# Attention and two MLPs on one core: the start made anew, the first MLP's products begun pair by pair, and idle products on TensorE

## The chip, the cores and the metric

The kernel runs on one core of one Trainium2 chip. The metric is the device time of one execution in microseconds, median of several runs; before the change it is 845.37 us (three runs, 844.19 to 846.44). The core's engines are TensorE (PE; PEld is its weight load), VectorE (DVE), ScalarE (ACT), GpSimd (POOL) and SyncE (SP, which here only issues DMAs). TensorE writes to PSUM, which has eight banks of 128 partitions by 512 f32 columns.

## The reference

Four batches, eight heads, 576 positions, head size 64. Scores get a bias from a running sum of gates and a causal mask; then come two MLPs on the 2304 tokens.

```python
def _attn_ref(q, k, v, s):
    B, H, S, D = q.shape                     # 4, 8, 576, 64
    scores = np.matmul(q, k.transpose(0, 1, 3, 2)) / np.sqrt(D)
    cum = np.cumsum(np.maximum(s, 0.0), axis=-1)
    bias = -(cum[:, :, :, None] - cum[:, :, None, :])
    scores = np.where(causal, -1e9, scores + np.minimum(bias, 0.0))
    attn = softmax(scores)
    return np.matmul(attn, v)

def _moe_ref(x, w_in, w_out, g_ln):          # 512 -> 1024 -> 512
    h = x @ w_in
    solu = h * softmax(h)
    return layernorm(solu) * g_ln @ w_out

def _moe2_ref(x, w_in, w_out):               # 512 -> 2048 -> 512
    h = x @ w_in
    return (h * np.clip(h + 3.0, 0.0, 6.0) / 6.0) @ w_out
```

Weights come as float64, which the kernel reads as pairs of 32-bit words and decodes on ScalarE and VectorE to a rounded high part and a low part. MLP products are made of three: high by high, low by high, high by low.

## The kernel before

The whole program is planned. Every step is entered in a list by `plan.add` with its engine, an estimated duration, what it reads and writes, buffers that it takes from a ring (`new`), a PSUM bank, and sometimes steps after whose start it may begin (`after`). `Plan.emit` schedules the list: each engine takes, of the steps that are ready by the estimates, the one that was entered first; a step that needs a PSUM bank waits until one is free. The instructions are then written engine by engine in that order, and on the chip each engine and each DMA queue works strictly in it.

Batch 0 is done in head pairs, 0 to 3. `load_qk` loads a pair's q and k (two DMAs of 144 KB each) on SP's queue; `prep_whole` transposes them on TensorE (12 products with the identity, L440) and copies them out (q on ScalarE at L445, k on VectorE at L447). `gate_rows` loads the gates s of all heads, takes the running sum on VectorE (L278 to L282), splits it in a high and a low part and writes the parts and rows of ones to the DRAM tensor `rows_d` (L286); `load_gates` reads four rows for each head back into the lower half of a 128-partition tile `whole`, whose other rows there are zero (L427). A score group of `qk_whole` (L583) is four f32 products: gate rows of the two heads of the pair (64 partitions each), then q by k of the two heads (64 partitions each). Scores of the first 256 positions ("early", t = 0, 1) come first, pair by pair (`pairs(False)`); the others ("late", t = 2, 3, 4) follow (`pairs(True)`).

Softmax: VectorE adds the mask and takes the maximum (L531), ScalarE takes the exponential (L543), VectorE the reciprocal of the sum (L639, L640), GpSimd scales (L644). TensorE transposes the result (L678), ScalarE or VectorE copies it out (L682), TensorE multiplies it by V (`av`, L707), and the product is copied to the x tile (L714). The first MLP works on tiles of 128 tokens: `ffn1_x` rounds a whole x tile to xh (VectorE, L794) and subtracts to xl (GpSimd, L798); `ffn1_h` adds up 24 products (L812: two halves f of w_in by four chunks kk by three); then come statistics, transposes (L878) and `ffn1_out` with w_out (L899). Chunk kk of x is what head pair kk gives. Tiles 0 and 1 are just the first 256 positions of batch 0.

`split64` loads and decodes one piece of a weight; for w_in (8 pieces, `load_w_in`) the load (512 KB) is issued from ScalarE's queue (L317), after the piece two before it is done; the steps of decoding are L323 (ACT), L327 and L331 (DVE), the high part L338 (DVE, first four) or L340 (ACT), the low part L347 (POOL). The 16 pieces of w_out follow in the same way. From batch 1 on, scores come from stacks of 128 rows in one f32r pass (L610), whose gate rows also come from `rows_d`. The second MLP (L1071, L1102) ends the program.

Of the kernel before, what the change touches and what calls it, by code (L numbers as in the profile page):

```python
# [37 lines left out]
HI_IN = 4  # L38
# [3 lines left out]
LAG = 2  # L42
DELAY = 3.5
# [4 lines left out]
class Plan:  # L48
# [45 lines left out]
    def emit(self):  # L94
# [17 lines left out]
        banks = [(0.0, b) for b in range(8)]  # L112
# [51 lines left out]
        for _, i in sorted(order):  # L164
            self.ops[i][2]()
# [23 lines left out]
def kernel(ctx, tc, q, k, v, s, w_in, w_out, g_ln, w2_in, w2_out, out):  # L189
# [53 lines left out]
    w_out_part(False)  # L243
# [21 lines left out]
    def gate_rows():  # L265

        s_sb = ap2.tile([P, S], F32, tag="y4", name="s_sb")[:NH]
        one = ap2.tile([P, S], F32, tag="y4", name="one")[:NH]
        cum = ap2.tile([P, NQ, 2, D], F32, tag="V", name="cum").rearrange("p c j d -> p (c j d)")[:NH, :S]  # L270
        pos = ap2.tile([P, PT_COLS], F32, tag="pt", name="pos", bufs=PT).bitcast(F32R)[:NH, : 2 * S]
        neg = ap2.tile([P, PT_COLS], F32, tag="pt", name="neg", bufs=PT).bitcast(F32R)[:NH, : 2 * S]

        def load():
            nc.sync.dma_start(out=s_sb, in_=s.rearrange("b h s -> (b h) s"))

        def sums():
            nc.vector.tensor_scalar_max(s_sb, s_sb, 0.0)  # L278
            nc.vector.tensor_tensor_scan(cum, one, s_sb, 0.0, ALU.mult, ALU.add)
            nc.vector.tensor_copy(pos[:, :S], cum)  # L280
            nc.vector.tensor_sub(pos[:, S:], cum, pos[:, :S].bitcast(F32))
            nc.vector.tensor_scalar_mul(neg, pos.bitcast(F32), -1.0)  # L282

        def put(i, r, src):
            dst = rows_d[:, i, r::2, :]
            nc.sync.dma_start(out=dst, in_=src)  # L286

        def zeros(j):
            whole_t[j] = ap1.tile([P, 4, S], F32, tag=f"stack{j}", name=f"whole{j}")
            nc.gpsimd.memset(whole_t[j][:, 2:4, :], 0.0)  # L290

        plan.add("SP", 0.45, load, writes=["s"], lag=2.0)
        plan.add("POOL", 2.2, lambda: nc.gpsimd.memset(one, 1.0), writes=["one"])
        plan.add("DVE", 3.0, sums, reads=["s", "one"], writes=["c"])
        ones = one.unsqueeze(1).to_broadcast([NH, 2, S])
        both = lambda c: c.bitcast(F32).rearrange("p (i s) -> p i s", i=2)
        for i, r, src, key in ((1, 0, both(pos), "c"), (0, 1, both(neg), "c"), (0, 0, ones, "one"), (1, 1, ones, "one")):
            plan.add("SP", 0.55, lambda i=i, r=r, src=src: put(i, r, src), reads=[key], writes=[f"rows/{i}{r}"], lag=2.0)
        for j in range(2):
            plan.add("POOL", 1.3, lambda j=j: zeros(j), writes=[f"zeros{j}"], new=[(f"stack{j}", 1, f"whole{j}")])  # L300

    def split64(plan, pool, src, hi, lo, name, key, scale=None, bufs=1, ring="", raws64=2, after=(), hi_dve=False, on_dve=(), behind=None, needs=(), home=()):
# [6 lines left out]
        w = f"raw_{name}"  # L309

        def load():
            T["raw"] = raw = pool_at().tile([P, n, 2], I32, tag="raw64", name=w, bufs=raws64)
# [8 lines left out]
        def high():  # L321
            T["a"] = pool_at().tile([P, n], F32, tag="dec_a", name=f"a_{name}", bufs=bufs)
# [870 lines left out]
```

## Time and profile before

| what | value |
|---|---|
| median of three runs | 845.37 us |
| profiled execution, its own time | 846.22 us |
| its span in the trace | 844.40 us |
| TensorE busy | 818.4 us (97%) |
| VectorE busy | 438.5 us (52%) |
| ScalarE busy | 399.4 us (47%) |
| GpSimd busy | 209.4 us (25%) |

The profile is that of one execution. An engine counts as busy while an instruction runs; the ends of TensorE's products are modelled, so shares close to 100% mean "no gap", not "at its peak". The page also cuts the span in 40 slices of 21.1 us each and gives the busy share of each in tenths, and the granted clock of TensorE in tenths of full speed. The chain of waits is followed back from the last instruction: at each step to what released it.

### The profile page before, as it was taken

What the parts mean: (1) busy time and instruction counts of PE and PEld (TensorE: products, weight loads), DVE (VectorE), ACT (ScalarE), POOL (GpSimd) and SP (SyncE); (2) the same over time, 40 slices, a digit from 0 to 9 for tenths busy, and PEclk for the clock granted to TensorE, in tenths of its full rate; (3) what the DMA queues carried; (4) which work ended last, traced back from release to release, by engine and by line L of the source; (5) the groups of instructions that cost most, each with busy time, mean ns of one, the idle gap of its engine ahead of it and who ended that gap; (6) DMA issues with size and microseconds to landing.
All of it is one profiled execution on the core that took longest, in us unless ns stands there. A gap on an engine that the chain in (4) does not pass through costs nothing.

```text
span 844.4 us, 13546 instructions
## 1 busy us (share of the span) xinstructions
PE 818.4 (97%) x4864; PEld 689.5 (82%) x4864; DVE 438.5 (52%) x1125; ACT 399.4 (47%) x928; POOL 209.4 (25%) x309
## 2 busy tenths in 40 slices
PE   4899999999999999999999999999999999999997
PEld 3565588898898889888999999998888888888886
DVE  4677887746855574749826982234222322222221
ACT  2575767755765575736636662244222422232222
POOL 1563643424632363327402220000000000000000
PEclk9899999999999999999999999999999999999999
DMA  6753596755646455223605640012000300010001
GB/s 172 180 152 110 120 209 152 176 120 130 129 118 137 98 129 120 65 99 121 193 32 194 214 148 1 1 62 88 1 1 0 100 1 0 1 50 1 0 1 50
DMA packets 95938, 77.52 MB, mean 92 GB/s; under 512 B 64288, under 2 KB 78112, under 8 KB 95872
## 3 DMA queue, kind: packets, MB, share of 16 engines
q1 hardware_dynamic: 93568, 68.27, 31.9%
q10 hardware_dynamic: 2304, 8.39, 3.1%
q8 instruction: 38, 0.62, 0.3%
q14 instruction: 28, 0.23, 0.1%
HBM read 45.38 MB, written 10.03 MB: 66 GB/s over the span
## 4 chain that ended last, share of the span: by engine, by line
PE 91%; DVE 4%; DMA 1%; POOL 1%; issue 1%; ACT 0%; POOLq 0%; DVEq 0%; SPq 0%; ACTq 0%
PE bank L1071 24%; PE bank L1102 24%; PE bank L899 11%; PE bank L812 11%; PE bank L707 6%; PE bank L678 5%; PE bank L610 5%; PE bank L583 3%; PE bank L878 2%; PE bank L473 1%; DMA stack<-HL12k 1%; DVE y L531 0%; DMA rows_d<-neg 0%; POOL y L626 0%; POOL y L644 0%
## 5 line engine op out<-in xcount | busy, mean ns | idle before, releaser
L1071 PE MATMUL bank<-x2h,w 128*128 128x512 f32 (+1 forms) x640 | 185.3, 370 | 0.0
L1102 PE MATMUL bank<-w,gh 128*128 128x512 f32 x576 | 178.8, 393 | 0.0
L1079 DVE SCALAR_TENSOR_TENSOR g<-g,bank 128x512 f32<-128x512 f32 (+1 forms) x80 | 50.6, 633 | 206.3 <-ACT g L1075 206.0
L1071 PEld LDWEIGHTS bank<-x2h,w 128*128 128x128 f32 x640 | 118.7, 188 | 18.7
L1075 ACT ACTIVATE g<-bank 128x512 f32<-128x512 f32 (+1 forms) x80 | 44.5, 556 | 178.8 <-PE bank L1071 178.7
L1102 PEld LDWEIGHTS bank<-w,gh 128*128 128x128 f32 x576 | 107.9, 188 | 21.9
L1071 PE MATMUL bank<-x2l,w 128*128 128x512 f32 (+1 forms) x320 | 118.5, 370 | 0.0
L1102 PE MATMUL bank<-w,gl 128*128 128x512 f32 x288 | 111.9, 391 | 0.0
L531 DVE CUSTOM_DVE_ANT_0 y<-bank,mask 96x288 f32<-96x288 f32 (+4 forms) x168 | 74.6, 467 | 57.3 <-PE bank L610 37.7
L543 ACT ACTIVATE y<-y,nmax 128x256 f32<-128x256 f32 (+4 forms) x140 | 83.4, 597 | 41.4 <-DVE nmax L531 29.9
L626 POOL TENSOR_SCALAR y<-y,rsum 128x128 f32<-128x128 f32 (+4 forms) x120 | 68.1, 589 | 103.7 <-DVE rsum L622 48.5
L899 PE MATMUL bank<-zh,w_out_h 128*128 128x256 f32 x288 | 82.8, 288 | 0.0
L899 PE MATMUL bank<-zl,w_out_h 128*128 128x256 f32 x288 | 81.2, 282 | 0.0
L899 PE MATMUL bank<-zh,w_out_l 128*128 128x256 f32 x288 | 81.2, 282 | 0.0
L1087 DVE TENSOR_TENSOR gl<-g,gh 128x512 fp32r<-128x512 f32 (+1 forms) x80 | 53.7, 671 | 43.4 <-ACT gh L1083 42.6
L1083 ACT CAST gh<-g 128x512 fp32r<-128x512 f32 (+1 forms) x80 | 46.2, 577 | 48.2 <-DVE g L1079 48.1
L1071 PEld LDWEIGHTS bank<-x2l,w 128*128 128x128 f32 x320 | 60.0, 188 | 8.3
L1102 PEld LDWEIGHTS bank<-w,gl 128*128 128x128 f32 x288 | 54.1, 188 | 12.1
L812 PE MATMUL bank<-w_in_h,xh 128*128 128x512 f32 x144 | 61.6, 428 | 0.8 <-DVE xh L794 0.8
L610 PE MATMUL bank<-stack 128*96 128x288 f32 (+4 forms) x288 | 57.8, 317 | 1.2 <-DMA stack<-HL12k 0.8
L812 PE MATMUL bank<-w_in_h,xl 128*128 128x512 f32 x144 | 57.4, 399 | 0.6 <-POOL xl L798 0.6
L812 PE MATMUL bank<-w_in_l,xh 128*128 128x512 f32 x144 | 57.4, 398 | 0.0
(220 smaller groups left out, 1360.9 us busy)
## 6 DMA issues: line engine op xcount, KB each, us to landing
raw_w2i<-in_moe_w_in_dram SPq DMA_DIRECT2D x16, 512.0 KB
raw_w2o<-in_moe_w_out_dram SPq DMA_DIRECT2D x16, 512.0 KB
rawq<-in_q_dram SPq DMA_DIRECT2D x32, 144.0 KB
rawk<-in_k_dram SPq DMA_DIRECT2D x32, 144.0 KB
x_d<-x2s SPq DMA_DIRECT2D x36, 128.0 KB
out_dram<-ob SPq DMA_DIRECT2D x18, 256.0 KB
raw_wi<-in_moe_w_in_dram ACTq DMA_DIRECT2D x8, 512.0 KB
raw_wo<-in_moe_w_out_dram ACTq DMA_DIRECT2D x8, 512.0 KB
```

The lines of the kernel that those rows point to most:

```text
L531: nc.vector.tensor_tensor_reduce(out=ys[h, t][:n, c0:c1], in0=bank(key)[:n, : c1 - c0], in1=mask[:n, 480 + n - w + c0 : 480 + n - w + c1], ...
L543: nc.scalar.activation(out=y[:n], in_=y[:n], func=AF.Exp, bias=nmax[:n, h, t : t + 1], scale=-1.0, accum_out=sums[:n, h, t : t + 1])
L610: nc.tensor.matmul(bank(key)[:n, : c1 - c0], lhsT=ss[:, 2 - 2 * m, ST[t] : w], rhs=ss[:, 3 - 2 * m, c0:c1], start=(m == 0), stop=(m == 1))
L626: nc.gpsimd.tensor_scalar(ys[h, t][:n], ys[h, t][:n], rsum[:n, h, t : t + 1], 1.0, ALU.mult, ALU.mult)
L707: nc.tensor.matmul(bank(key)[j * D : (j + 1) * D, lo - c0 : c1 - c0], lhsT=vs[v_key(p, a)][:n, jj, j, :], rhs=pts[pt_key(2 * p + j, a)][:n ...
L812: nc.tensor.matmul(bank(key), lhsT=xs[i][m // 2][:, kk, :], rhs=(w_in_l if m == 1 else w_in_h)[:, kk, f * 512 : (f + 1) * 512], start=(kk ...
L899: nc.tensor.matmul(bank(key)[:, : 2 * P], lhsT=w_out_at(w, kk)[:, m * P : (m + 1) * P], rhs=z[:, kk, :], start=(kk == 0 and i == 0), stop= ...
L1071: nc.tensor.matmul(bank(key)[:, :w], lhsT=wt[:, a, 0, c * P : (c + 1) * P], rhs=x[:, c, :w], start=(c == 0 and i == 0), stop=(c == KDM - 1 ...
L1079: nc.vector.scalar_tensor_tensor(out=gg, in0=gg, scalar=6.0, in1=bank(key)[:, :w], op0=ALU.min, op1=ALU.mult)
L1083: nc.scalar.copy(gh[:, :w], gg[:, :w])
L1087: nc.vector.tensor_sub(gl[:, :w], gg[:, :w], gh[:, :w].bitcast(F32))
L1102: nc.tensor.matmul(bank(key), lhsT=g_t[ci, m][1 + i // 2][:, t * P : (t + 1) * P], rhs=w2[m][:, i % 2, 1, :], start=(m == 0 and i == 0), s ...
```

## The change

1. **Gates of batch 0 on the chip.** The first eight heads' s come by a DMA that is the first on ScalarE's queue. `places` makes, from the identity, a small matrix that has two ones for each head; four f32 products (`own`, 288 columns, 8 rows) spread s to two rows in each of four strips of 32 partitions. ScalarE clips (`clip`), VectorE takes the running sum (`total`) and turns the two rows of a strip to sum and one; ScalarE writes the key rows (`keys`). The sum is no longer split in high and low. One tile `whole` holds the gates of two pairs, and a head's gate product has 32 partitions. `load_gates` is gone. The `rows_d` tensor, which batches 1 to 3 need, is made later by `all_rows`, after `po3_0` (the early product of pair 3 with V) has begun.
2. **q and k of pairs 1, 2, 3** are loaded at the start, into buffers that the first MLP uses later (`raw_home`), so without waiting for the pair before.
3. **w_in** is loaded by SP's queue, into the home of w_out's first part and decoded in place there; w_out's decoding begins when that is done. The high part is VectorE's for the first two pieces, not four.
4. **x of tiles 0 and 1.** For batch 0's early part `av` no longer copies to x; ScalarE rounds each pair's product to xh straight from PSUM and VectorE subtracts to xl. `ffn1_h` of tiles 0 and 1 waits for chunk kk alone, not for the whole tile.
5. **Idle products.** `emit` fills 60% of TensorE's planned idle time from 1 to 24 us of the plan with products of the identity by itself (taken as bf16, 256 columns), 46 in all, into bank 7, which the plan gives to others only from 24 us on; nothing reads them.
6. Estimates of score groups and loads are changed, which moves the order everywhere.

The core of the diff:

```diff
-HI_IN = 4
+HI_IN = 2
+FILL_FROM, FILL_TO, FILL_N, FILL = 1.0, 24.0, 256, 0.6
...
-        banks = [(0.0, b) for b in range(8)]
+        banks = [(0.0, b) for b in range(7)] + [(FILL_TO, 7)]
...
-        for _, i in sorted(order):
-            self.ops[i][2]()
+        todo = [(start, i, self.ops[i][2]) for start, i in order]
+        free = FILL_FROM
+        for start, i in sorted((start, i) for start, i in order if self.ops[i][0] == "PE" and start < FILL_TO):
+            todo += [(free + k * fill_us, -1, fill) for k in range(int(FILL * (start - free) / fill_us))]
+            free = max(free, start + self.ops[i][1])
+        for _, _, f in sorted(todo, key=lambda x: x[:2]):
+            f()
...
+        def own(i, c):
+            n = S // 2
+            nc.tensor.matmul(bank(f"own{i}_{c}")[:, :n], lhsT=spread[:, i].rearrange("h g r -> h (g r)"), rhs=s_first[:, c * n : (c + 1) * n], start=True, stop=True)
...
+            nc.scalar.activation(out=cums[i][:, c * n : (c + 1) * n], in_=bank(f"own{i}_{c}")[:, :n], func=AF.Relu)
...
+            nc.vector.tensor_tensor_scan(cums[i], one, cums[i], 0.0, ALU.mult, ALU.add)
+            nc.vector.tensor_scalar(whole_t[i][:, 2, :], cums[i], at[:, 1:2], at[:, 0:1], ALU.mult, ALU.add)
...
+            nc.scalar.activation(out=whole_t[i][:, 3, :], in_=cums[i], func=AF.Identity, scale=at[:, 0:1], bias=at[:, 2:3])
...
+        plan.add("ACT", 0.4, lambda: nc.scalar.dma_start(out=s_first, in_=s[0]), writes=["s0"], lag=2.3)
...
-        return whole_t[p % 2][j * D : (j + 1) * D, 2:4, :]
+        r = (2 * (p % 2) + j) * (P // 4)
+        return whole_t[p // 2][r : r + P // 4, 2:4, :]
...
-            issue = nc.sync if behind is None else nc.scalar
+            issue = nc.sync if behind is None or raw_at else nc.scalar
...
+            if b == 0 and a == 0:
+                for i in range(2):
+                    def high(i=i, key=key):
+                        nc.scalar.copy(xs[i][0][:, hp, :], bank(key)[:, i * P : (i + 1) * P])
+                    def low(i=i, key=key):
+                        nc.vector.tensor_sub(xs[i][1][:, hp, :], bank(key)[:, i * P : (i + 1) * P], xs[i][0][:, hp, :].bitcast(F32))
...
-        plan.add("PE", 0.7, mm, reads=[f"xs{i}/h", f"xs{i}/l"] + W_IN[kk, f], writes=[key],
+        plan.add("PE", 0.7, mm, reads=[f"xs{i}/{x}{kk if i < 2 else ''}" for x in "hl"] + W_IN[kk, f], writes=[key],
...
+    def keep_clock():
+        x = ident.bitcast(BF16)
+        nc.tensor.matmul(banks[7][:, :FILL_N], lhsT=x[:, :P], rhs=x[:, :FILL_N], start=True, stop=True)
```

What this does to the order is seen at three places. The line numbers are those of each kernel: L512, L661, L756, L785 and L903 of the change are L440, L583, L678, L707 and L812 of before.

TensorE's first work before: the transposes of pair 0's q and k, the first score group, then pair 1's q.

```order
L440 MATMUL bank0_96<-ident_60,rawq0_119 128x96 x3
L440 MATMUL bank1_97<-ident_60,rawq0_119 128x96 x3
L440 MATMUL bank2_98<-ident_60,rawk0_122 128x96 x3
L440 MATMUL bank3_99<-ident_60,rawk0_122 128x96 x3
L583 MATMUL bank4_100<-whole0_125 128x128
L583 MATMUL bank5_101<-whole0_125 128x128
L583 MATMUL bank4_100<-HL0_137 128x128
L583 MATMUL bank5_101<-HL0_137 128x128
L440 MATMUL bank6_102<-ident_60,rawq1_147 128x96 x3
```

The same place in the change, from the last of the first ten idle products (L1268) on; L287 is `own`.

```order
L1268 LDWEIGHTS ident_60
L1268 MATMUL bank7_101<-ident_60 128x256
L287 MATMUL bank0_94<-start_t_109 128x288
L287 MATMUL bank1_95<-start_t_109 128x288
L287 MATMUL bank2_96<-start_t_109 128x288
L287 MATMUL bank3_97<-start_t_109 128x288
L512 MATMUL bank4_98<-ident_60,rawq0_119 128x96 x3
L512 MATMUL bank5_99<-ident_60,rawq0_119 128x96 x3
```

The spreading products and idle products have come ahead of pair 0's transposes; the first score group now stands behind the transposes of pairs 0 and 1 and of half of pair 2's q.

TensorE where the first MLP begins, before: the last early transposes (L678) and late scores are done, pair 3's product with V (L707) is made, and the products of tile 0 follow one another.

```order
L707 MATMUL bank5_101<-pt6a_496,V3a_420 64x256
L707 MATMUL bank5_101<-pt7a_501,V3a_420 64x256
L707 MATMUL bank5_101<-pt6a_496,V3a_420 64x128
L707 MATMUL bank5_101<-pt7a_501,V3a_420 64x128
L473 MATMUL bank0_96<-ident_60,rawq4_354 128x96 x3
L473 MATMUL bank2_98<-ident_60,rawq4_354 128x96 x3
L812 MATMUL bank5_101<-w_in_h_82,xh0_555 128x512
L812 MATMUL bank5_101<-w_in_l_83,xh0_555 128x512
L812 MATMUL bank5_101<-w_in_h_82,xl0_556 128x512
```

In the change, behind pair 3's early scores (L661, `whole1`):

```order
L661 MATMUL bank2_96<-whole1_208 128x256
L661 MATMUL bank3_97<-whole1_208 128x256
...
L903 MATMUL bank5_99<-w_in_h_82,xh0_388 128x512
L903 MATMUL bank5_99<-w_in_l_83,xh0_388 128x512
L903 MATMUL bank5_99<-w_in_h_82,xl0_389 128x512
L756 MATMUL bank1_95<-ident_60,yf2_303 128x128 x3
L756 MATMUL bank6_100<-ident_60,yf3_304 128x128 x3
L661 MATMUL bank7_101<-whole0_163 128x384
L661 MATMUL bank1_95<-whole0_163 128x384
L661 MATMUL bank7_101<-HL0_152 128x384
L661 MATMUL bank1_95<-HL0_152 128x384
```

Three products of tile 0, for chunk 0 alone, stand between the early and the late scores of pair 0; the others of tiles 0 and 1 follow in threes between score groups, transposes and products with V, all ahead of the first transposes of the late part.

SP's queue at the start, before (L275 loads s, L286 writes `rows_d`, L427 reads it):

```order
L275 DMA s_sb_110<-in_s_dram 32x576
L395 DMA rawq0_119<-in_q_dram 96x6x64 x2
L395 DMA rawk0_122<-in_k_dram 96x6x64 x2
L286 DMA rows_d_71<-one_111 32x2x576 x2
L286 DMA rows_d_71<-pos_113 32x2x576
L286 DMA rows_d_71<-neg_114 32x2x576
L395 DMA rawq1_147<-in_q_dram 96x6x64 x2
```

In the change (`rawqz`, `rawkz` hold pair 1's and then pair 2's):

```order
L466 DMA rawq0_119<-in_q_dram 96x6x64 x2
L466 DMA rawk0_122<-in_k_dram 96x6x64 x2
L466 DMA rawqz_131<-in_q_dram 96x6x64 x2
L466 DMA rawkz_132<-in_k_dram 96x6x64 x2
L366 DMA raw_w_in0_142<-in_moe_w_in_dram 128x1024
```

Pair 1's loads have moved up directly behind pair 0's, and the first w_in piece stands on this queue, ahead of pair 2's.

## Rows read from the trace of the kernel before

**Rows 1.** The page, busy share by engine, and slices of 21.1 us.
```profile
PE 818.4 (97%) x4864; PEld 689.5 (82%) x4864; DVE 438.5 (52%) x1125; ACT 399.4 (47%) x928; POOL 209.4 (25%) x309
...
PE   4899999999999999999999999999999999999997
...
PEclk9899999999999999999999999999999999999999
```

**Rows 2.** Stretches: length, busy us of each engine, granted clock, DMA share, GB/s.
```profile
0.00:15.00 15.00, 2.39 (x12) 1.89 (x13) 7.48 (x9) 2.99 (x5) 4.20 (x13) 1.00 0.73 199
15.00:31.00 16.00, 14.47 (x80) 10.74 (x82) 7.56 (x33) 7.90 (x28) 6.69 (x10) 0.83 0.64 145
31.00:62.25 31.25, 28.18 (x171) 18.44 (x172) 23.55 (x77) 20.07 (x53) 17.15 (x20) 0.92 0.65 169
62.25:109.30 47.05, 45.11 (x321) 29.15 (x320) 38.16 (x109) 31.27 (x75) 23.18 (x33) 1.00 0.50 123
109.30:844.40 735.10, 728.25 (x4286) 629.25 (x4284) 361.75 (x898) 337.19 (x768) 158.13 (x234) 1.00 0.32 83
```

**Rows 3.** Chain of waits up to 34 us: start, duration, what (f32 products count twice).
```profile
0.72 2.00 DMA s_sb<-in_s_dram
...
5.19 1.36 DVE cum L279
...
8.61 4.17 DMA rows_d<-neg
...
12.93 1.93 DMA whole<-rows_d
...
15.00 1.57 PE bank L583 x8
...
17.73 2.01 PE bank L583 x8
...
30.96 1.48 PE bank L707 x8
...
33.24 0.50 PE bank L440 x6
33.74 2.75 PE bank L583 x16
```

**Rows 4.** Timeline up to 23 us: start, duration, engine, line, operation.
```profile
1.14 0.29 POOL masks.py:199 TENSOR_SCALAR_AFFINE_SELECT ident<-ident 128x128 f32<-128x128 f32 x1
...
4.66 1.19 PE L440 MATMUL bank<-ident,rawq 96*128 96x96 f32 x6 [4.66 <-DMA rawq<-in_q_dram]
...
5.41 0.89 ACT L445 ACTIVATE HL<-bank 128x288 f32<-128x288 f32 x2 [3.20 <-PE bank L440]
...
22.44 0.59 PE L583 MATMUL bank<-HL 64*128 64x256 f32 x4
```

**Rows 5.** Chain of waits again, later pieces.
```profile
54.69 1.27 POOL xl L798
...
56.01 6.25 PE bank L812 x19
62.25 2.17 PE bank L678 x24
...
79.39 1.14 PE bank L583 x8
80.54 0.90 PE bank L812 x3
...
82.58 0.38 PE bank L678 x3
82.97 0.73 PE bank L812 x3
...
171.12 2.89 PE bank L899 x24
```

**Rows 6.** Timeline, the first product with w_out.
```profile
109.34 0.28 PE L899 MATMUL bank<-zh,w_out_h 128*128 128x256 f32 x1
```

More of the change, by code (lines that the diff above doesn't have):

```diff
@@ L292, in gate_rows @@
[L292 to L298, printed above, removed]
@@ L299, in gate_rows @@
-        for j in range(2):
-            plan.add("POOL", 1.3, lambda j=j: zeros(j), writes=[f"zeros{j}"], new=[(f"stack{j}", 1, f"whole{j}")])
-    def split64(plan, pool, src, hi, lo, name, key, scale=None, bufs=1, ring="", raws64=2, after=(), hi_dve=False, on_dve=(), behind=None, needs=(), home=()):
+        one = ap2.tile([P, S], F32, tag="y4", name="one")
+        start_t = ap2.tile([P, PT_COLS], F32, tag="pt", name="start_t", bufs=PT)[:H]
+        s_first = start_t[:, :S]
+        at = const.tile([P, 3], F32, name="at")
@@ new lines, in gate_rows, with gates @@
+        plan.add("POOL", 1.9, lambda: nc.gpsimd.memset(one, 1.0), writes=["one"])
+        plan.add("DVE", 1.4, places, writes=["at"])
+        def gates(i):
+            for c in range(2):
+                key = f"own{i}_{c}"
+                plan.add("PE", 0.3, lambda i=i, c=c: own(i, c), reads=["s0", "at"], writes=[key], bank=key)
+                plan.add("ACT", 0.45, lambda i=i, c=c: clip(i, c), reads=[key], writes=[f"cum{i}/{c}"], new=[("e", 2, f"cum{i}")] if c == 0 else [])
+            plan.add("DVE", 2.0, lambda i=i: total(i), reads=[f"cum{i}/0", f"cum{i}/1", "one", "at"], writes=[f"gates{i}/q", f"cum{i}/t"], new=[(f"stack{i}", 1, f"whole{i}")])
+            plan.add("ACT", 0.7, lambda i=i: keys(i), reads=[f"cum{i}/t"], writes=[f"gates{i}/k"])
@@ L304, in split64 @@
+    def split64(plan, pool, src, hi, lo, name, key, scale=None, bufs=1, ring="", raws64=2, after=(), hi_dve=False, on_dve=(), behind=None, needs=(), home=(), raw_at=None, a_at=None):
         n = 512
@@ L366, in load_w_in, with raw_at @@
         c %= KDM
[L367 to L368 removed]
+        i = c + f.start // 128
+        def raw_at():
+            if i < 2:
+                w1_raw[i] = w1p.tile([P, KFF - LATE_OUT, DM], F32, tag=f"w_out_{'hl'[i]}0", name=f"raw_w_in{i}").rearrange("p c n -> p (c n)")
+            o = (i % 4 // 2) * 1024
+            return w1_raw[i % 2][:, o : o + 1024].bitcast(I32).rearrange("p (n w) -> p n w", w=2)
+        first = [lambda: plan.add("ACT", 0.0, lambda: None, writes=["raws/"], new=[("wout", 1, "raws")])] if i == 0 else []
+        return first + split64(plan, dec, w_in[c * P : (c + 1) * P, f], w_in_h[:, c, f], w_in_l[:, c, f], f"wi{c}_{f.start // 512}", "win",
+                               behind=[], hi_dve=i < HI_IN, raw_at=raw_at, a_at=lambda: w1_raw[i % 2][:, 2048:])
     def load_w_out(c):
@@ L546, in exps @@
             plan.add("DVE", 0.2, both, reads=[f"nmax{h}_{NQ}"], writes=[f"nmax{h}_{t}"])
-        plan.add("ACT", act(w, 0.46), exp, reads=[f"nmax{h}_{t}"] + [f"{y_key(h, t)}/{c0}" for c0, _, _ in pieces], writes=[f"{y_key(h, t)}/e", f"sums{h}_{t}"])
+        plan.add("ACT", act(w, 0.46), exp, reads=[f"nmax{h}_{t}"] + [f"{y_key(h, t)}/{c0}" for c0, _, _ in pieces], writes=[f"{y_key(h, t)}/e", f"sums{h}_{t}"],
+                 after=[f"rawx/{H - 1}_1/e"] if h < H and ST[t] >= CUT else [])
     def pieces_of(t):
```

177 lines of the change are left out of this document (117 added, 60 removed).

## The prediction

> **What bounds the kernel now.** I read the page's busy shares and the granted clock in slices first [rows 1]: TensorE is nearly full from the third slice on, so what can be gained lies at the start. The table of stretches [rows 2] splits it. Up to 15.0 us TensorE works 2.39 us; from 15 to 31 it works 14.47 of 16, from 31 to 62.25 28.18 of 31.25, from 62.25 to 109.3 45.11 of 47.05, and after that 728.25 of 735.1. So it idles 19.1 us before 109.3 and 6.85 after it. Part of the busy time is half speed: granted 0.83 and 0.92 in the second and third stretch are 2 x 0.17 x 16 = 5.4 and 2 x 0.08 x 31.25 = 5.0 us at 1.2 GHz.
>
> The chain of waits [rows 3] says why the start is late: s lands at 2.72, its running sum is taken on VectorE (1.36 us), the parts are written to DRAM (4.17 us) and read back (1.93 us), and only at 15.00 the first score products run. [...] I take that as the low level; by 22.44, where two of those 256-column products took 0.59 [rows 4], it is over. The first pair's product with V begins at 30.96. The first MLP begins when its whole x tile is rounded and split: the xl of 1.27 us at 54.69 releases the long run of MLP products at 56.01 [rows 5]. I use three marks: first product with V (30.96), first transposes of the second half (62.25), first products with w_out (109.34) [rows 3, 5, 6].
>
> **Up to the first product with V.** Removed are the trip through DRAM, its four DMAs ahead of pair 1's q on SP's queue, and the w_in DMAs beside it. Added is a chain on the chip. s of batch 0 goes first on ScalarE's queue; in before 2.00 us passed from issue to landing [rows 3], so 2.7. The identity is made at 1.14 + 0.29 = 1.43 [rows 4]. Ten idle products stand ahead of the first real one. No bf16 product is in the trace; the nearest are 24 of 256 columns in 2.89 us [rows 5], 0.12 each, 0.24 at the low level: TensorE is through with them at 2.7 to 3.9. I take 3.9, where the clock was low in before. The four products that spread s (288 columns, f32) have no row: if they ran as the paired score products do, 288 columns cost 0.26 (high) or 0.56 (low); alone, at most twice that, so 0.26 to 1.13. I take 0.8, the middle towards the low level: the second ends at 5.5, the fourth at 7.1. Then ScalarE's clip (0.45, half of the 0.89 for two of 288 columns [rows 4]), the scan (1.36 [rows 3]) and a scaled copy on VectorE (between 0.45 and 1.36; 0.75): query rows at 8.1. The key rows are on ScalarE behind pair 1's q copies. TensorE first transposes q0, k0 and q1, three times 0.50 to 1.19, with a filler product between: 9.9. Two copies 0.89, key rows 0.7: the first score product at 11.5 instead of 15.00 (10.5 if the clock is up, 13.4 if it is low throughout).
>
> It also has pair 2's q transpose ahead of it in TensorE's order, and so that DMA: five loads of q or k (295 KB each), one of w_in (524 KB) and s (18 KB) are 2.02 MB, at 199 GB/s [rows 2] 10.1 us, just in time. ScalarE's queue no longer issues w_in; SP's carries it between the q and k loads, so a late load holds up every later V and k.
>
> From the first score product to the first product with V before took 15.96 us, of which TensorE was busy 14.5, and about 6 + 5.4 us of that at the low level. If the products between keep the clock up, up to 6 us of TensorE's time goes; softmax on the other three engines stands in the same chain, so I take 3.0 (between 0 and 6). The first product with V then begins at 11.5 + 13.0 = **24.5, 6.5 us earlier** (20.5 to 29.4). The 36 other idle products cost nothing as long as the real ones behind them wait for softmax; were that cover gone, 36 x 0.12 to 0.24 = 4.3 to 8.6 us.
>
> **From there to 62.25.** Now both tiles' 48 MLP products stand among the score products, each pair's as its x slice is done; before only tile 0's 24 came, at the end. TensorE's sum in full speed: 48 products at 0.73 for three [rows 5], 11.7; two pairs' late scores, 11,520 columns at 0.895 ns, 10.3; pair 3's early scores 1.4; four pairs' V products at 0.74 (half of the 1.48 at the low level [rows 3]), 3.0; 18 transposes at 0.09 (24 in 2.17 [rows 5]), 1.6; six at 0.083, 0.5: 28.5.
>
> To that comes a cost that the words of the change don't tell. Gate rows now lie in 32-row strips, so each score group goes from two 32-row products to two 64-row ones; before all four used 64 rows. The chain shows what a step between such shapes costs: three MLP products take 0.90 us behind the 64-row score products and 0.73 behind transposes [rows 5], 0.16 more. Ten groups here, with four places where two groups follow each other, are 14 x 0.16 = 2.2 us. The Trainium skill (TensorEngine Tiling (Array Packing), Key Properties) says that changing the tiling mode, not just the tile, drains the engine. By that rule the step costs something in every group, and the trace agrees with 0.16 us; by the page's other promise, that tiles work independently, it would cost nothing.
>
> So 30.7 of work, and idle time: the same stretch idled 3.07 us before; with MLP products at hand, though with one PSUM bank fewer in the plan at first, I take 2.3. 33.0 us against 31.3: **1.7 us lost**, and the mark falls at 57.5. VectorE is no bound: it was busy 23.55 of 31.25, loses the x copies and roundings and gains eight small subtractions, the sums for the DRAM rows (some 4 us, moved from the start) and in-place decoding.
>
> **From 62.25 to 109.34.** TensorE's 45.11 us lose tile 1's 24 products (5.85) and gain 11 steps (1.8): 41.1, 6.0 less than the stretch took. But VectorE is busy 38.16 of 47.05 here and its work stays. Between 6.0 (TensorE still the bound) and 0 (softmax and decoding are) I take **3.0 us gained**. After the mark the work is the same and TensorE 99% busy: 0.
>
> **Sum.** -6.5 + 1.7 - 3.0 = -7.8 us. The profiled execution took 846.22 with a span of 844.40; the median of the three times is 845.37, 0.85 below it, and the 7.8 come off the median: 837.6 us.
>
> **Rivals.**
> Steps between strips are free: then 2.2 us, about 1 of the last stretch and 0.4 of the first come back: 834.0. For it speaks that both shapes divide the rows alike; against it the 0.90 beside 0.73.
> The second stretch of work gives it back: VectorE, 81% busy, sets the pace once tile 1's products are gone, 0 instead of 3.0: 840.6. Against it: TensorE was 96% busy there.
> Slower, the clock stays low: if the idle products do not lift TensorE, they cost 46 x 0.24 = 11.0, the four spreads 3.4, 48 early transposes 9.6, three pairs' early scores 9.0 with 1.0 of steps, transposes 1.6: 35.6 after 1.5, so the first product with V at 37.1, 6.1 late, and the sum is +6.1 + 1.7 - 3.0: 850.2. It decides if the rise comes after some 24 us. Against: in before it came between 17.73 and 22.44, 3 to 7 us after 15.00, under scores and transposes without gaps, and here TensorE starts at 1.5.
> Slower too, 32-row products of two heads do not run side by side: 14,592 columns (half of all those of four pairs' scores) cost their 0.895 ns twice, 13.1 us, some 9.4 of it seen: 847.0. No row shows 32-row strips.
> It does not do what it says: DMAs on SP's one queue hold pairs back so that MLP products come no earlier: about 845.
>
> **How the numbers follow.** Forecast 0.44, free steps 0.24, given back 0.14, low clock 0.08, strips alone 0.06, nothing 0.04. Times from 829.5 (first stretch 10 early and free steps) to 844.0 hold eight in ten. A run tells this kernel from no change at 0.3%, 2.5 us. Faster: 0.44 + 0.24 and most of "given back", 0.77; slower 0.13; within 0.10.
>
> **What would show it.** In the profile of the changed kernel: first score product at 10.5 to 13.4; the transposes' pace before it (0.50 or 1.19 for six) tells the clock; first product with V at 20.5 to 29.4; MLP products from about 27 instead of 54; three MLP products or a score group 0.16 longer than by columns alone tells the steps; the marks at about 57.5 and 101.5. Wrong would be the sum if TensorE idles over 4 us between the first two marks, or over 5 after the second.

## The result: slower, and why the profile after says so

The changed kernel takes 850.78 us (median of 13 runs, 848.66 to 859.50), the kernel before 845.54 (13 runs): ratio 1.0081, with a 95% interval of 1.0053 to 1.0108. Forecast were 837.6 us and a gain of 0.9%; by the medians it is a loss of 0.6%, 5.2 us. Ratios here are over all executions and not of the medians, but four of pad32's twelve executions, near 860 us, and one of before_pad's eleven, 1350.6 us, are left out of theirs as belonging to a slower state at a lower granted clock, while three of the changed kernel's, near 858 us, count.

The profiled execution is the longest of the 13 (859.50 us, span 857.5), with a mean granted clock of 0.990; ten of the 13 lie between 848.66 and 853.67 us, at 0.994 to 1.000. So where TensorE's clock is concerned the profile shows more than the median run lost.

The page, against [rows 1]: TensorE is full from the first slice on, as the change wants, but it is busy 841.5 us instead of 818.4, and the granted clock falls in the fourth slice.

```profile
PE 841.5 (98%) x4918; PEld 695.5 (81%) x4918; DVE 436.6 (51%) x1132; ACT 405.9 (47%) x944; POOL 205.5 (24%) x307
...
PE   9999989999999999999999999999999999999998
...
PEclk9997999999999999999999999999999999999999
```

The stretches with the boundaries of [rows 2] (length, busy us of each engine, granted clock, DMA share, GB/s). Up to 31 us TensorE idles only for the first 1.49 us, and from 62.25 to 109.3 the granted clock is 0.85, which is 2 x 0.15 x 47.05 = 14 us at 1.2 GHz; before had 1.00 there.

```profile
0.00:15.00 15.00, 13.51 (x59) 10.26 (x59) 6.22 (x10) 7.13 (x14) 2.21 (x11) 1.00 1.13 192
15.00:31.00 16.00, 16.00 (x117) 10.95 (x115) 10.77 (x43) 9.24 (x32) 7.76 (x11) 1.00 0.91 239
31.00:62.25 31.25, 31.01 (x169) 17.52 (x168) 22.47 (x66) 20.10 (x58) 16.94 (x22) 1.00 0.41 115
62.25:109.30 47.05, 43.53 (x270) 23.99 (x271) 35.46 (x111) 29.23 (x71) 18.77 (x29) 0.85 0.45 113
109.30:857.50 748.20, 737.50 (x4314) 632.81 (x4310) 361.69 (x904) 340.16 (x772) 159.78 (x236) 1.00 0.32 82
```

TensorE's timeline at the start, against [rows 3, 4] (start, duration, line, what; L1268 are the idle products, L287 the products that spread s, L661 the scores, L785 the products with V). Seven idle products still take 0.23 us each at 19.35, five at 21.55 take 0.14: only between the two the pace (columns per us) doubles, although TensorE has had no gap since 1.49. The first product with V comes at 29.31; the chain of waits, which [rows 3] are from, has 29.38 for it against 30.96, 1.58 us earlier.

```profile
1.49 2.32 PE L1268 MATMUL bank<-ident 128*128 128x256 bf16 x10 [1.49 <-POOL halfs L226]
3.73 4.20 PE L287 MATMUL bank<-start_t 8*128 8x288 f32 x8
...
13.66 0.80 PE L661 MATMUL bank<-whole 32*128 32x128 f32 x4
...
19.35 1.62 PE L1268 MATMUL bank<-ident 128*128 128x256 bf16 x7
...
21.55 0.71 PE L1268 MATMUL bank<-ident 128*128 128x256 bf16 x5
...
27.20 2.18 PE L661 MATMUL bank<-whole 32*128 32x128 f32 x16
29.31 0.43 PE L785 MATMUL bank<-pt0a,V0a 128*64 128x256 f32 x1
```

The chain of waits around the second mark (L756 are transposes, L327 to L335 the running sums for the DRAM rows). VectorE's queue holds the sums ahead of the reading of the last score products (yl L605): it waits for GpSimd's memsets until 58.32, sums for 3.91 us and is through at 63.48. TensorE, which had MLP products up to 62.7, stands until 64.66, and its 18 transposes behind that take 3.27 us, where 24 took 2.17 in [rows 5].

```profile
56.31 1.59 POOL y L722 x2
57.90 0.19 POOL rawqz L327
...
58.32 3.91 DVE rawqz L333
...
62.73 0.75 DVE rawqz L335
63.48 0.66 DVE w_out_l L394
...
64.66 3.27 PE bank L756 x18
```

Further on the chain has a copy by DMA that TensorE did not wait for before: the scores of pair 5 (L688) stand until its k (HL5k) is in the stack.

```profile
118.18 5.04 DMA stack<-HL5k
123.21 1.60 PE bank L688 x6
```

### The profile page after: what moved, and what is told of

The parts are those of the page before. It is cut to its first block, busy times and chain, and to the rows that moved or that the text cites. A ratio compares the mean times of both kernels' runs of the same rounds, so it can differ in the third digit from the quotient of the medians.

```text
span 857.5 us, 13664 instructions
## 1 busy us (share of the span) xinstructions
PE 841.5 (98%) x4918; PEld 695.5 (81%) x4918; DVE 436.6 (51%) x1132; ACT 405.9 (47%) x944; POOL 205.5 (24%) x307
## 4 chain that ended last, share of the span: by engine, by line
PE 93%; DVE 3%; DMA 1%; POOL 1%; issue 0%; ACT 0%; SPq 0%; POOLq 0%; DVEq 0%; ACTq 0%
PE bank L1206 23%; PE bank L1175 23%; PE bank L990 11%; PE bank L903 10%; PE bank L785 6%; PE bank L756 5%; PE bank L688 5%; PE bank L661 4%; PE bank L969 2%; PE bank L543 1%; PE bank L1268 1%; PE bank L512 1%; DMA stack<-HL12k 1%; DMA stack<-HL5k 1%; DVE y L605 1%; PE bank L287 0%
## 5 line engine op out<-in xcount | busy, mean ns | idle before, releaser
L605 DVE CUSTOM_DVE_ANT_0 y<-bank,mask 128x128 f32<-128x128 f32 (+4 forms) x164 | 73.1, 470 | 60.1 <-PE bank L688 47.2
L617 ACT ACTIVATE y<-y,nmax 96x576 f32<-96x576 f32 (+4 forms) x136 | 81.6, 601 | 37.0 <-DVE nmax L605 28.6
L688 PE MATMUL bank<-stack 128*96 128x288 f32 (+4 forms) x288 | 57.9, 320 | 5.2 <-DMA stack<-HL5k 3.8
L903 PE MATMUL bank<-w_in_h,xh 128*128 128x512 f32 x144 | 61.6, 428 | 0.3 <-ACT pt4a L760 0.2
L903 PE MATMUL bank<-w_in_l,xh 128*128 128x512 f32 x144 | 57.1, 396 | 0.0
L903 PE MATMUL bank<-w_in_h,xl 128*128 128x512 f32 x144 | 57.1, 396 | 0.0
```

The lines of the kernel that those rows point to most:

```text
L605: nc.vector.tensor_tensor_reduce(out=ys[h, t][:n, c0:c1], in0=bank(key)[:n, : c1 - c0], in1=mask[:n, 480 + n - w + c0 : 480 + n - w + c1], ...
L617: nc.scalar.activation(out=y[:n], in_=y[:n], func=AF.Exp, bias=nmax[:n, h, t : t + 1], scale=-1.0, accum_out=sums[:n, h, t : t + 1])
L688: nc.tensor.matmul(bank(key)[:n, : c1 - c0], lhsT=ss[:, 2 - 2 * m, ST[t] : w], rhs=ss[:, 3 - 2 * m, c0:c1], start=(m == 0), stop=(m == 1))
L903: nc.tensor.matmul(bank(key), lhsT=xs[i][m // 2][:, kk, :], rhs=(w_in_l if m == 1 else w_in_h)[:, kk, f * 512 : (f + 1) * 512], start=(kk ...
```

## Experiments: the idle products and the first pairs

My first theory was that the clock comes up near 20 us whatever TensorE does, so that the idle products only cost. The profile of each kernel is that of one execution.

**no_fill**, the idle products alone undone:

```diff
-FILL_FROM, FILL_TO, FILL_N, FILL = 1.0, 24.0, 256, 0.6
+FILL_FROM, FILL_TO, FILL_N, FILL = 1.0, 24.0, 256, 0.0
```

> The 46 idle products on the identity are left out; their PSUM bank stays reserved up to the same planned time, all else is as in the changed kernel. Theory (the start is paced by a clock that rises near 20 us whatever TensorE does, so the idle products only cost their own time at the low level): four-product score groups still at the low pace up to about 20 us, first product with V between 28 and 29.5 (29.38 with them), time 848 to 851 against 850.8. Rival (the idle products bring the clock up or hold it): the rise comes at 22 us or later or the clock falls again before 31 us, first product with V after 30.5, time 853 or more.

Measured: 867.91 us, ratio 1.0266 (1.0226 to 1.0306), 17 us slower than with them. One mark of the theory held: the first product with V comes at 29.21, as early as with the idle products. The theory itself fell. TensorE's timeline of this kernel: it works without a gap from 12 us on, and yet a product of 512 columns takes 0.63 us up to 51.49; only at 53.66 it is 0.39.

```profile
29.21 0.69 PE L785 MATMUL bank<-pt0a,V0a 128*64 128x256 f32 x1
...
51.49 0.63 PE L903 MATMUL bank<-w_in_h,xl 128*128 128x512 f32 x1
...
53.66 0.39 PE L903 MATMUL bank<-w_in_l,xh 128*128 128x512 f32 x1
```

What TensorE did in these 50 us were score products of 32 and 64 rows, transposes and, ahead of the rise, the first MLP products; with the idle products between them it came to the high pace between 11 and 21 us, though in some profiles it fell again (see below). So up to the first product with V the idle products gained nothing that they did not cost; what they were worth came after it, where no_fill ran at half pace for 20 us more.

**whole_x**, the pair-by-pair part alone undone (`reads` of the products of tiles 0 and 1 name all four slices of x):

> The first MLP's products of tiles 0 and 1 wait again until all four slices of x are there, instead of beginning pair by pair; all else as in the changed kernel. Theory (products at hand fill TensorE's idle time between 31 and 55 us, but the time is then lost behind VectorE's queue at 55 to 65 us): TensorE idles 3 to 6 us more between 31 and 55, loses less at 62 to 65, time 850 to 854. Rival (beginning pair by pair is itself the loss, since the MLP products stand ahead of score groups that softmax waits for): 845 to 848.

Measured: 855.85, ratio 1.0116 (1.0084 to 1.0147), 3 us slower than the changed kernel by the ratios and 5 by the medians, with intervals that overlap. So beginning pair by pair seems to be worth something: without it TensorE is busy 28.28 us of the third stretch, where the changed kernel has 31.01. The granted clock, 0.89 and 0.95 in the second and third stretch against 1.00, is a weaker sign, since up to 31 us the order of TensorE is the same in both.

**before_fill**, the idle products alone put into the kernel before:

> The kernel before with the idle products alone: a bank is kept from the plan up to 24 us of planned time and idle products of 256 columns are put into TensorE's planned idle time by the same rule; no other part of the change. Theory (dense idle products lift the clock earlier and hold it): two 256-column products of a pair at the fast pace from the first on, granted clock 1.00 between 25 and 32 us, first product with V at 26 to 29 instead of 30.96, time 840.5 to 843.5 against 845.2. Rival (what they gain is lost behind them, or the clock falls again in the waits): 844 to 847.

Measured: 854.04, ratio 1.0098. Both numbers missed. The clock did come up early (six transposes in 0.66 us at 6.64, where [rows 4] have 1.19), but it was not held: TensorE stood from 10.75 to 17.56, and behind that six transposes took 1.22 us again. The first scores came at 17.6 instead of 15.0, and the late scores of the first pair waited for gate rows at 37 us. **before_bank7** takes the idle products out again and leaves the plan with a bank less:

> The kernel before with one PSUM bank kept from the plan up to 24 us, as in before_fill, and no idle products. Theory (the bank less makes another plan, in which the first pair's late scores wait for their gate rows from DRAM at 36 to 39 us, and that is what cost before_fill its 8.5 us): 852 to 858, the same waits. Rival (the idle products are what made it slower): 844 to 847.

Measured: 846.37, ratio 1.0002 (0.9991 to 1.0012). My theory of the plan fell too; the idle products themselves go with the loss. In the chains of the two the trip through DRAM is longer with them, first before_fill, then before_bank7 (start, duration, what):

```profile
8.62 5.60 DMA rows_d<-neg
...
14.61 3.82 DMA whole<-rows_d
```

```profile
8.62 4.57 DMA rows_d<-neg
...
13.34 2.29 DMA whole<-rows_d
```

Why it is longer was not tried. The changed kernel has no such trip at the start.

## Experiments: the sums, the strips and the place

**ones_row**, a written row of ones for the sum instead of one column read again and again:

> The running sum of the 32 gate rows for the DRAM copy takes its ones from a written row of 576 instead of one column read again and again; the memset on GpSimd grows from 192 to 768 columns, nothing else changes. Theory (VectorE, held by that sum at 58 to 62 us, makes TensorE wait at 62 to 65): the sum falls from 3.9 us to about 1.4, the first late transposes begin near 62 to 62.5 instead of 64.66, TensorE's granted clock falls less after it, time 846 to 848.5, with a smaller spread. Rival (TensorE would have waited there for something else, the GpSimd normalising or the tops): 850 to 851, mark at 64 or later.

Measured: 852.81 (848.07 to 857.02), no gain. The sum did get shorter, but the casts behind it got longer, as its chain shows:

```profile
63.40 2.48 DVE rawqz L333
...
65.90 0.84 DVE rawkz L334
...
66.77 1.18 DVE rawqz L335
```

In the changed kernel the last two took 0.46 (L334) and 0.75. From the first step of the sums to the reading of the scores (L605) VectorE's queue took 6.95 us instead of 7.08, so the sum's gain was lost behind it. (The late transposes began at 69.13; in this profile TensorE's pace, up at 11 us, fell again, with a granted clock of 0.50 from 22 to 38 us.) GpSimd normalises beside the sums (3.98 us from 63.36). A sum of that length took 1.36 us in [rows 3], where GpSimd did nothing. The Trainium skill (GPSIMD Engine Reference, 1. Specifications) says that GpSimd's way to SBUF is shared with VectorE, and that VectorE instructions with two SBUF inputs contend with it; 1.36 alone and 2.48 beside it agree. The edit did not take GpSimd away, so this cause is argued and not shown.

**rows_early** moves the sums instead:

```diff
-writes=["rawz/q1", "rawz/s"], lag=2.0, after=["po3_0"])
+writes=["rawz/q1", "rawz/s"], lag=2.0, after=["po0_0"])
...
+            all_rows()
             mix(second[0], early[: len(early) // 4])
-            all_rows()
```

> The changed kernel with the running sums for the DRAM rows taken earlier: their load is let go when the first pair's product with V begins instead of the fourth's, and they stand ahead of the late scores of pair 0 in the plan, so that VectorE does them at some 33 to 42 us and not at 57 to 63.5. Theory (there they hold up the tops and the copies of the transposes, TensorE idles 2 to 2.4 us, and its granted clock falls after that): no idle time of over 1 us at 60 to 66, first late transposes 2 to 4 us earlier than 64.66, time 845.5 to 849. Rival (GpSimd's normalising is what the late transposes wait for, the sums only fill the time): the idle time stays, 850 to 852.

Measured: 848.25 us, ratio 1.0030 (1.0018 to 1.0042), and a spread of 3.6 us instead of 10.8. The first late transposes begin at 61.18, TensorE's gap at 62 is gone, and the granted clock is 1.00 from 62.25 to 109.3:

```profile
60.95 0.39 PE L903 MATMUL bank<-w_in_h,xl 128*128 128x512 f32 x1
61.18 1.00 PE L756 MATMUL bank<-ident,y 128*128 128x128 f32 x9
...
62.75 1.55 PE L756 MATMUL bank<-ident,y 128*128 128x128 f32 x15
```

```profile
62.25:109.30 47.05, 43.99 (x327) 27.56 (x326) 38.69 (x128) 34.03 (x84) 21.33 (x31) 1.00 0.61 145
```

Two more things go with it. A stop has come at 42 us, where VectorE is late now, but the granted clock stays 1.00 behind it:

```profile
43.70 0.50 PE L903 MATMUL bank<-w_in_h,xh 128*128 128x512 f32 x1 [1.75 <-DVE nmax L605]
```

And the wait for pair 5's stacked rows is gone: between 66 and 135 us TensorE stands nowhere longer than 1.21 us, where the changed kernel stood for 3.79 and ones_row, wide_rows, whole_x, no_fill and pad32, which all have the sums late, for 2.7 to 3.0. So the 2.5 us that this run gains by the medians (4.3 by the ratios) are shown to come from the place of the sums; how they are shared between the stop at 62 and the wait of pair 5 is not.

**wide_rows** gives the gate products 64 rows:

```diff
-        r = (2 * (p % 2) + j) * (P // 4)
-        return whole_t[p // 2][r : r + P // 4, 2:4, :]
+        return whole_t[p // 2][j * D : (j + 1) * D, 2:4, :]
```

> The gate products of the first four pairs read 64 rows of the gate tile instead of 32, so that both products of a score group have one shape; it changes which rows are multiplied (other heads' gate rows come in), so it gives the time of that shape and not the scores. Theory (a step between 32 and 64 rows costs 0.18 to 0.38 us in each of the 24 score groups, part of it hidden): a 288-column group falls from 1.32 to about 1.14 us, a 480 one from 1.96 to 1.78, time 845 to 848. Rival (TensorE waits there for softmax anyway, so the steps cost nothing that is seen): groups shorter, time 850 to 851. Second rival (steps are free, the longer groups are only later clocks): groups as long as now.

Measured: 847.54, ratio 1.0034 (1.0015 to 1.0053), 3.2 us less than the changed kernel by the medians and 4 by the ratios, for all steps. Two groups of 128 columns in a row take 1.58 us, where the changed kernel needs 2.18 at the same pace; the three steps within them (32 to 64, 64 to 32, 32 to 64 rows) cost 0.20 each.

```profile
24.43 1.58 PE L660 MATMUL bank<-whole 64*128 64x128 f32 x16
25.94 0.43 PE L784 MATMUL bank<-pt0a,V0a 128*64 128x256 f32 x1
```

Even so no gain on the kernel before was left. Matched by instruction, the last 2,200 matmuls, which are the same in both, took 451.3 us from start to start in the changed kernel and 449.3 before. The two differ in the place of their tiles: a new constant of 12 bytes (`at`), counted here as 32 in each partition, moves every tile of that side of the on-chip memory. No trace shows addresses; the runs below bear out the count. **pad32** adds an unread one:

```diff
     halfs = const.tile([P, 1], F32, name="halfs")
+    pad = const.tile([P, 1], F32, name="pad")
```

> The changed kernel with one more constant of four bytes a partition, which nothing reads: it takes 32 bytes, and every tile of the attention's side and the second MLP's weights and inputs begins 32 bytes further on, at 32 beyond a multiple of 64 as in the kernel before, where in the changed kernel they begin at multiples of 64 (the change's own new constant had moved them by 32). Nothing else changes. Theory (the place makes every matmul about 1 ns slower, 229 ns from start to start in the middle where before has 227, 2.0 us over the last 2,200 matmuls): that difference goes, the last 2,200 matmuls take 449.3 us as before instead of 451.3, time 847 to 849 against 850.8. Rival (it is the order or the semaphores of the changed program): 451.3 stays and the time is 850 to 852.

Measured: 849.20 us (842.65 to 860.52), ratio 1.0015 (0.9993 to 1.0037): the spread hides it, but its fastest run is 6.0 us under the changed kernel's fastest. **before_pad** is the same in the kernel before:

> The kernel before with the same unread constant, so that the tiles begin at multiples of 64 bytes, as in the changed kernel. Theory of the place: every matmul about 1 ns slower, the last 2,200 matmuls 2.0 us longer, time 847 to 849 against 845.2. Rival: no difference, 845 to 845.6.

Measured: 847.52, ratio 1.0019 (1.0010 to 1.0028): slower by 1.8 us without one instruction changed. **before_pad64** takes it one step further, to the addresses of pad32:

> The kernel before with an unread constant of 64 bytes: the second MLP's weights and inputs lie at the same addresses as in pad32 and early_pad32. Theory of the place: the last 2,200 matmuls take 445.7 us as there, instead of 449.3, and the time is 841 to 842.5 against 845.3. Rival (the 445.7 belongs to the changed program): 449 to 451 us, time 845 to 848.

Measured: 842.08, ratio 0.9959 (0.9946 to 0.9973). The profile shows it in the time from the first to the last of the second MLP's products with its input, which one line groups (first and last start at its end), here of the changed kernel and of pad32:

```profile
L1175 PE MATMUL bank<-x2h,w x640: 332/389/421, 434.4 to 844.7; 128*128 128x512 f32 x96, 128*128 128x384 f32 x64
```

```profile
L1176 PE MATMUL bank<-x2h,w x640: 331/389/423, 430.5 to 835.4; 128*128 128x512 f32 x96, 128*128 128x384 f32 x64
```

| place of the tiles, in bytes from that of the kernel before | from first to last, us |
|---|---|
| 0 (before) | 408.5 |
| +32 (changed kernel, before_pad) | 410.3, 410.1 |
| +64 (pad32, before_pad64) | 404.9, 404.8 |
| +96 (early_pad64) | 410.6 |

The others agree with their place: no_fill, ones_row, wide_rows, whole_x and rows_early 410.3, before_fill and before_bank7 408.4, early_pad32 and the three runs made from it without moving a tile (early_alt, early_fill, early_alt_nofill) 404.9. At +64 `at` with four bytes more and, in the kernel before, 36 bytes alone come to the same place and the same time.

## Experiments: the parts put together

**early_pad32** is rows_early and pad32 together:

> Both edits together: the running sums for the DRAM rows taken at 33 to 42 us, and the unread constant of 32 bytes. Theory (two separate causes, the place worth 5.6 us in the last 2,200 matmuls, which took 445.7 us with it and 451.3 without, and the sums worth 1.5 to 2.5 us and the falls of the clock behind them): they add up, 840.5 to 843.5, faster than the 845.7 of the kernel before, with a spread under 5 us. Rival (pad32's fast runs owed it to something else, since its runs lay between 842.65 and 860.5): 846 to 849.

Measured: 843.22 (840.61 to 843.63), ratio 0.9963 (0.9949 to 0.9977): the two add up, and the spread is 3 us. **early_pad64** (a constant of nine columns instead of one) leaves the place as the only difference:

> As early_pad32, with an unread constant of 64 bytes, so that the tiles begin at multiples of 64 again, one step of 32 further. If what counts is whether a tile begins at a multiple of 64, the last 2,200 matmuls take some 451 us again and the time is 846 to 849; if it is the place itself, step by step, they take some other time than 445.7 and 451.3.

Measured: 847.49, ratio 1.0030 (1.0016 to 1.0044): 4.3 us for 32 bytes. Whether a tile begins at a multiple of 64 does not decide it alone: the kernel before and pad32 both lie at 32 beyond one and differ by 3.6 us.

**early_alt** adds to early_pad32 that every second score group takes its two kinds of product in the other order:

```diff
-            for m in range(2):
+            kinds = (turn_of[0], 1 - turn_of[0])
+            turn_of[0] = kinds[1]
+            for m in kinds:
...
-start=(m == 0), stop=(m == 1))
+start=(m == kinds[0]), stop=(m == kinds[1]))
```

> As early_pad32, and every second score group of the first four pairs begins with the product that the group ahead of it ended with (two 32-row or two 64-row products), so that where groups follow each other half of the steps between the two shapes go. Theory (a step costs 0.1 to 0.2 us, as wide_rows' 3.2 us for all of them says): two groups in a row some 0.1 to 0.2 us shorter, 0.5 to 1.5 us in all, 840 to 842.5. Rival (the step inside a group is what costs, or a step in either direction is hidden): no more than 0.3 us from early_pad32.

Measured: 840.02 us (838.02 to 841.28), ratio 0.9932 (0.9917 to 0.9947). It is faster than both kernels as they stand. Two groups of 128 columns take 1.98 us instead of 2.18:

```profile
24.83 1.98 PE L665 MATMUL bank<-whole 32*128 32x128 f32 x16
26.73 0.43 PE L789 MATMUL bank<-pt0a,V0a 128*64 128x256 f32 x1
```

That is one step less, 0.20 us, wherever two groups follow each other, some ten times: 2 of the 3.2 us. Its profiled run also kept the high pace from 12 us on; how much of the rest is that is open.

**early_fill** has 80 idle products instead of 46:

> As early_pad32, with idle products in all of the planned idle time up to 24 us instead of 60% of it: 80 instead of 46, the plan itself unchanged. Theory (the clock rises once TensorE has had dense full-array work behind it for some us; in before_fill 25 idle products from 1.49 us on had it up at 6.5, while in the changed kernel it came between 11.4 and 20.8): rise before 11 us, first product with V before 27 us instead of 29.38, 0 to 3 us faster than early_pad32. Rival (the additional 34 products delay the real work by their own 0.12 to 0.23 us each): 1 to 5 us slower than early_pad32.

Measured: 845.15 (841.32 to 847.23), ratio 0.9989 (0.9975 to 1.0003), 1.9 us slower than early_pad32. The pace did come up early, at 5 us (four products that spread s in 2.29 us instead of 4.20), but it was low again from 9 to 12 and from 16 to 19.7, and the first product with V came at 29.91. More of them is not better.

```profile
5.22 2.29 PE L288 MATMUL bank<-start_t 8*128 8x288 f32 x8
...
18.07 1.86 PE L1269 MATMUL bank<-ident 128*128 128x256 bf16 x11
```

**early_alt_nofill** has none:

> early_alt (840.0) without the 46 idle products, the plan unchanged. Theory (32-row and 64-row score products alone keep TensorE busy but do not bring its clock up, which in no_fill stayed at the low pace to 52 us): low pace until the MLP products, at 45 us or later, time 852 to 860. Rival (no_fill's loss was the sums and the falls behind them): 840 to 845.

Measured: 846.48, ratio 1.0009, 6.4 us slower than early_alt, not the 12 to 20 expected. The low pace again lasts through full work, but only to some 37 us:

```profile
35.40 0.63 PE L907 MATMUL bank<-w_in_h,xl 128*128 128x512 f32 x1
...
43.79 0.42 PE L907 MATMUL bank<-w_in_h,xl 128*128 128x512 f32 x1
```

## Why the prediction was wrong

Three steps of the sum failed: the stretch up to the first product with V (6.5 us forecast, 1.6 gained), "VectorE is no bound" behind it, and "after the mark the work is the same: 0". The marks are those of the profiled execution, whose span is 13.1 us longer than before's: 1.6 gained, then 4.0, 1.9 and 8.8 lost. The median run lost 5.2 us; how that splits on the stretches no trace shows. What single edits were worth is known: 1.8 us for the place (before_pad), 2.5 to 4.3 for the place of the sums in the order (rows_early), 3.2 to 4 for the steps (wide_rows).

- **First mark, forecast 24.5: 29.4.** The first score product came at 13.66 (11.5 forecast, 13.4 the end of its range). The ten idle products were priced right (through at 3.73, 3.9 forecast), the spreading products took 1.05 each where I had taken 0.8. But then I counted three groups of transposes and one idle product ahead of the first score product, where the order of the change shows four groups and half of a fifth, with six idle products (1.3 us) among them; and I expected a wait for key rows, but TensorE stood nowhere: its own queue set the time. From there to the first product with V it took 15.65 us and not 13.0. Two things stand in it, each as large as the 2.65 missing: the pace doubled only at 20.8, which by my estimate lost 2.6 us (half of the 5.3 us of score products and transposes up to there), and 30 idle products kept TensorE for 4.4 us. "The 36 other idle products cost nothing as long as the real ones behind them wait" failed with its condition, since nothing waited.

  The pace was read from one execution (a rise 3 to 7 us after TensorE's start, kept up by the products between). Other profiles with the same start differ:

  | profile | pace doubled at, us | low again | first product with V, us |
  |---|---|---|---|
  | changed kernel, rows_early, early_pad64 | 20.8 to 21.3 | no | 29.30 to 29.54 |
  | ones_row, pad32, whole_x, early_pad32 | 11.4 to 13.3 | for 3 to 17 us, beginning between 15 and 24 | 28.65 to 30.55 |
  | wide_rows, early_alt | 12 to 13.7 | no | 25.94, 26.73 |
  | no_fill, early_alt_nofill (no idle products) | 52, 37 | no | 29.21, 29.44 |

  Only where the pace came up early and stayed did the stretch take the forecast 13.0 us (12.3 and 12.8); why it stayed in two and fell in four is open.
- **The steps between strips were priced about right:** 0.16 us forecast, 0.20 measured; 2.2 + 1.8 us in all, 3.2 to 4 measured with wide_rows. The Trainium skill (TensorEngine Tiling (Array Packing), Key Properties) says that a change of mode drains the engine; these 0.20 us agree.
- **"VectorE is no bound" failed.** I had the sums as "some 4 us, moved from the start" and looked at VectorE's busy share. What counted was their place in its queue: from 56.99 to 63.48 nothing else came through, and the sums met GpSimd's normalising. From the first mark to the second it took 35.3 us (33.0 forecast), 2.0 of it TensorE's stop behind the sums. So of the 7.2 us that the second mark was late (64.66, 57.5 forecast) 4.9 come from the first mark and 2.3 from here. The stop lies within the bound of 4 that I had set as a sign; the granted clock behind it was not in the sum at all.
- **Third stretch, forecast 3.0 us gained: 1.9 lost** (49.0 us from 64.66 to the first product with w_out at 113.64, 47.1 before), with 14 us of it at 1.2 GHz. Some 3 us of that come right behind the stop at 62; ones_row, wide_rows, pad32, whole_x and no_fill have such a stop there and such a fall, and the six kernels with the sums early have neither. The other 10 us, from 78 to 89, are in no other profile, and what brought them is open. pad32, the same program at another place, took 44.6 us here (64.90 to 109.53), 2.5 gained: this step of the sum was about right, and its loss belongs to the longest execution.
- **"After the mark the work is the same: 0" failed.** It took 743.9 us instead of 735.1. Parts of the 8.8 us are TensorE's wait for pair 5's stacked rows (3.8), half of the 3 us or so at the low level behind it, and 1.8 to 2.0 for the place of the tiles, which no row of the kernel before could show, but the diff did: it adds a tile to the constants. The rest is not traced. The sign that I had set here, 5 us of idle time after the second mark, was no test: before idles 8.8 us there already.
- **The rivals.** "The clock stays low" gave 850.2, near the time measured, but not by its mechanism: it wanted the first product with V at 37.1, and even no_fill, at the low pace to 52 us, had it at 29.21. "Steps are free" is refuted by wide_rows. "32-row products not side by side" is refuted: in a group of 480 columns the 32-row half takes 0.97 us (35.75 to 36.72 in the changed kernel) and the 64-row half 0.98. "It does not do what it says" is refuted too: the MLP products begin at 32.21 us and not at 54.65. "VectorE sets the pace" was nearest, one stretch too late.
- **The range.** Its lower end was added up wrong: ten us early and free steps give 830.5, not 829.5.

Put together, against the kernel before: the changed kernel 1.0081, with the place mended 1.0015, with the sums moved too 0.9963, with one step less wherever two score groups follow each other 0.9932 (0.9917 to 0.9947). With the same place the kernel before stands at 0.9959 (0.9946 to 0.9973). So with place and sums mended the change only draws level, and with the steps mended too it gains some 0.3%, at the edge of the intervals; the two were not timed side by side.

## What to carry to other kernels

When work moves, price its place in the queue of the engine that does it, and what runs beside it then; a busy share of 75% says nothing of a queue that stands for 6 us. Filler work is free only while the engine would otherwise wait: count what stands behind it. Look at every new tile for what it shifts, and compare the pace of work that did not change before explaining the rest. A kernel whose start depends on the clock needs several runs before its time means anything, and several profiles before a stretch of one does.

## What the runs showed of the hardware that I had not expected

- 32 bytes more or less in the place of the tiles moved the second MLP by 2 to 6 us of 405 (408.5 at 0, 410.3 at +32, 404.9 at +64, 410.6 at +96), the same in all kernels at one place; which of its tiles it is was not tried.
- TensorE stayed at half pace through full work, to 52 us in no_fill and 37 in early_alt_nofill. The profile's granted clock reads 1.00 in these stretches; that the pace is half shows only in the durations (in no_fill six transposes of 128 columns 1.48 us that later take 0.82, a product of 512 columns 0.63 that later takes 0.39).
- After a stop of 2 us at 62 us the granted clock was 0.66 over the five us from 65, and five other kernels with a stop of 1.9 to 3.0 us at that place fell in the same way; after a stop of 1.75 us near 42 us (rows_early and the five runs made from it) it stayed at 1.00. It was also 0.50 from 80 to 85 in the changed kernel, with TensorE busy and no stop over 0.33 us since 64.66; no other profile has that.
